# Prefix sums from a softplus split in two fp32r parts, with reordered loads, tokens and conversions, in a gated attention and MLP kernel

## The chip, the cores and the metric

The kernel runs on one core of one Trainium2 chip. The metric is the time of one execution on the device in microseconds; the median over three runs counts.

## What is computed

Per head, a gated linear attention with a state of 48 x 48: `state = f[t] * state + k[t] v[t]^T`, `y[t] = q[t] state`, with `f = 1 / (1 + exp(-f_logit))`; 4 batches, 8 heads, 768 tokens. The heads are joined to 384 channels. Then follows a token mix and a first MLP:

```
xt = x.transpose(0, 2, 1)
h = xt @ U @ V
u = x + h.transpose(0, 2, 1)
x = u + np.maximum(u @ w_ch1, 0.0) @ w_ch2
```

and a second MLP with a convolution of three taps over the tokens and a gate: `h = relu(x @ w_in)`, `out = (h * sigmoid(conv(h))) @ w_out`. The weights come in as 64-bit floats.

## The kernel before

**Chunks.** The attention runs over 24 chunks (6 per batch) of 128 tokens, in a loop over i. What is called chunk i below is iteration i. The logarithms of the gates are summed within a chunk by a matrix product with the triangle `tri`: `prefix(g)` multiplies `tri` by the softplus `sp` of chunk g into `n`, ScalarE makes `a = Exp(-n)` and `b = Exp(n)` of it, and `hats()` multiplies q by a and k by the clamped b (`qh`, `kh`), on VectorE for the first six chunks and on GpSimd from then on. `turn` transposes qh and kh on TensorE and ScalarE copies them out. `scores(i)` are eight products of keys and queries (`s`), `mask` multiplies them by the triangle on VectorE (`p`), and `out_chunk(i)` collects `y` in strips of 32 columns: first the queries with the state of the chunks before (`y<-qT,w`, not in the first chunk of a batch), then the masked scores with the values (`y<-p,v`), and last, unless the chunk is the last of its batch, the products `kv` that feed the next state. `state_end` adds kv to the state on VectorE (`wtmp`) and GpSimd scales it (`w`) by the prefix end of the chunk. That end is the last row of a; `ends` sends it to DRAM and `ends_back` fetches it over the partitions (`ga`).

**Tokens.** `tokens` transposes a finished chunk (`xt`, three transposes); ScalarE rounds it to fp32r (`xh`) and VectorE makes the rest (`xl`). `mix_in` multiplies both by U (`z`); when a batch is complete, `mix_z` prepares the sum and `mix_out` adds the product with V (`mix`), two products per chunk over three chunks.

**How values are split.** The large products run in fp32r, as three products of a high and a low part. `split` rounds on ScalarE (line 105) and subtracts on another engine (line 79). Products in plain fp32 are written as one `mm` call and appear in the trace as two matmuls.

**The order.** Every engine executes in program order, and the program is written out by hand, without a scheduler. In iteration i the loads of f for chunk i + 4, of k and q for i + 3 and of v for i + 2 are issued on SP first, then `ends_back`; `prefix(i + 2)` and `mix_next` follow, the scores, the hats, the masks, the token transposes, the transpose of the next queries, the gates (Exp and Ln of `f`, lines 547 and 548) of chunk i + 3, `ends(i + 2)`, `out_chunk`, and the transpose of the next keys between two mix products. `slot` deals out the steps that turn 64-bit weights into fp32r (VectorE, lines 128 to 138), some ahead of the masks and some behind the gates:

```
def slots(i):
    return (0, 6) if i == 1 else (0, 0) if i < 5 else (2, 2) if i < 8 else (1, 2)
```

**The seam.** In chunk 23 the first MLP's input is split; `up1` and `down1` follow, and `hooks` insert the last token mix between the products of the first `up1`. The two MLPs, some 504 us, run from fp32r parts throughout.

Of the kernel before, what the change touches and what calls it, by code (L numbers as in the profile page):

```python
# [35 lines left out]
def kernel(  # L36
# [168 lines left out]
    def mlps(ms, banks, pieces, late, checks, hooks):  # L205
# [226 lines left out]
        split1(0, 1, (nc.gpsimd, nc.vector))  # L432
        yield
# [60 lines left out]
    tri = gc.tile([128, 128], F32, name="tri")  # L494
    ga = gc.tile([128, NG, NP], F32, name="ga")
# [18 lines left out]
    sps = {}  # L514
# [34 lines left out]

    def prefix(g):  # L550
        n = bank(6, [128, DM], "n")
        mm(n, tri, sps.pop(g).rearrange("p h d -> p (h d)"), True, True)
# [108 lines left out]
    def out_chunk(g):  # L661
# [104 lines left out]
    with tc.manual_schedule():  # L766
# [7 lines left out]
        nc.vector.memset(ga, 1.0)  # L774
        for t, x in ((a_t[0], 1.0), (q_t[0], 0.0), (k_t[0], 0.0)):
# [58 lines left out]
        def slots(i):  # L834
            return (0, 6) if i == 1 else (0, 0) if i < 5 else (2, 2) if i < 8 else (1, 2)
# [31 lines left out]
        for i in range(1, NG):  # L867
            load_of(f"f{i + 4}")
            for x in "kq":
                load_of(f"{x}{i + 3}")  # L870
            load_of(f"v{i + 2}")
            if i < NG - 1:
# [3 lines left out]
            if EARLY_GATES <= i < NG - 3:  # L876
                gate_max(i + 3)
# [20 lines left out]
            if i < EARLY_GATES:  # L898
                gate_max(i + 3)
# [14 lines left out]
            if i < NG - 3:  # L914
                gates(i + 3)
# [233 lines left out]
```

## Time and profile before

| | |
|---|---|
| median of 3 runs | 654.48 us (653.5 to 655.22) |
| profiled execution, its own time | 654.5 us |
| its span | 652.8 us |
| TensorE busy | 641.3 us (98%) |
| VectorE / ScalarE / GpSimd busy | 424.9 / 275.2 / 145.6 us |
| granted TensorE clock | 0.998 of full speed |

The profile is one execution as the hardware recorded it. Busy time is the time in which an engine has at least one instruction under way; matrix products are pipelined, so a busy TensorE need not be one at its peak, and the distance between two like products tells more than their duration. PE is TensorE's product, PEld its weight load, DVE VectorE, ACT ScalarE, POOL GpSimd, SP the engine that issues the transfers. An idle time in square brackets stands before an instruction, with what ended it.

### The profile page before, as it was taken

How to read it: one execution, taken by the hardware profiler on the slowest of the kernel's cores; microseconds unless marked ns; L12 is line 12 of the kernel's file. 1: busy time of each engine (PE TensorE's matmuls, PEld its weight loads, DVE VectorE, ACT ScalarE, POOL GpSimd, SP SyncE). 2: the span in 40 equal slices, each digit the busy share in tenths (PEclk: the TensorE clock that was granted, in tenths of full speed). 3: DMA queues.
4: the chain of work that ended last, by engine and by line, in shares of the span. 5: the costliest groups of instructions: out<-in, count | busy, mean ns of one | idle time of the engine just before them, and what ended most of it. 6: DMA issues, size and time to landing. Idle time of an engine off the chain costs nothing.

```text
span 652.8 us, 12695 instructions
## 1 busy us (share of the span) xinstructions
PE 641.3 (98%) x5146; PEld 559.3 (86%) x5146; DVE 424.9 (65%) x663; ACT 275.2 (42%) x524; POOL 145.6 (22%) x181
## 2 busy tenths in 40 slices
PE   8999999999999999999999999999999999999995
PEld 6788778777888788888888888889999999999995
DVE  4868876566666665666665334226988777787762
ACT  5779677853223232222232111123544644634533
POOL 1176678441222222111112000001120110110000
PEclk9999999999999999999999999999999999999999
DMA  9988898810333330222220466100000200200202
GB/s 181 171 163 168 168 175 155 148 51 2 96 98 96 98 97 1 73 73 73 72 73 0 126 193 190 48 0 2 1 0 1 73 2 0 74 2 1 72 1 78
DMA packets 132661, 50.56 MB, mean 77 GB/s; under 512 B 112900, under 2 KB 128285, under 8 KB 132595
## 3 DMA queue, kind: packets, MB, share of 16 engines
q1 hardware_dynamic: 132594, 49.67, 31.2%
q8 instruction: 42, 0.69, 0.4%
q14 instruction: 25, 0.20, 0.1%
HBM read 44.89 MB, written 4.76 MB: 76 GB/s over the span
## 4 chain that ended last, share of the span: by engine, by line
PE 94%; DVE 2%; ACT 1%; issue 1%; DMA 0%; POOL 0%; POOLq 0%
PE a L76 38%; PE b L76 38%; PE y L76 5%; PE s L76 4%; PE n L76 2%; PE kTp L598 2%; PE xt L688 1%; PE qTp L598 1%; PE z L76 1%; PE mix L76 1%; PE kv L76 1%; DVE p L619 1%; DMA f<-in_f_logit_dram 0%; ACT sp L548 0%; PE row L76 0%
## 5 line engine op out<-in xcount | busy, mean ns | idle before, releaser
L262 ACT ACTIVATE rh<-a 128x512 fp32r<-128x512 f32 x72 | 43.1, 599 | 221.9 <-PE a L76 217.6
L263 DVE SCALAR_TENSOR_TENSOR rl<-a,rh 128x512 fp32r<-128x512 f32 x72 | 49.8, 692 | 109.1 <-ACT rh L262 109.0
L76 PE MATMUL a<-uh,w1l 128*128 128x512 f32 x216 | 84.4, 391 | 0.0
L76 PE MATMUL a<-uh,w1h 128*128 128x512 f32 x216 | 84.2, 390 | 0.0
L76 PE MATMUL a<-ul,w1h 128*128 128x512 f32 x216 | 84.1, 389 | 0.0
L76 PE MATMUL b<-rh,w2l 128*128 128x512 f32 x216 | 84.1, 389 | 0.0
L76 PE MATMUL b<-rh,w2h 128*128 128x512 f32 x216 | 84.0, 389 | 0.0
L76 PE MATMUL b<-rl,w2h 128*128 128x512 f32 x216 | 84.0, 389 | 0.0
L76 PE MATMUL b<-woh,w1h 128*128 128x384 f32 x264 | 70.4, 335 | 0.0
L318 ACT ACTIVATE c<-c 128x768 f32<-128x768 f32 x31 | 26.3, 847 | 62.4 <-DVE c L348 62.4
L76 PEld LDWEIGHTS a<-uh,w1l 128*128 128x128 f32 x216 | 40.5, 188 | 10.0 <-POOL w1l L79 1.8
L76 PE MATMUL a<-w2h,winh 128*128 128x384 f32 x192 | 49.0, 336 | 0.0
L76 PEld LDWEIGHTS b<-woh,w1h 128*128 128x128 f32 x264 | 48.0, 188 | 0.0
L76 PEld LDWEIGHTS b<-rh,w2h 128*128 128x128 f32 x216 | 40.6, 188 | 8.5
L76 PEld LDWEIGHTS b<-rh,w2l 128*128 128x128 f32 x216 | 40.5, 188 | 8.5
L76 PEld LDWEIGHTS b<-rl,w2h 128*128 128x128 f32 x216 | 40.5, 188 | 8.4
L76 PEld LDWEIGHTS a<-ul,w1h 128*128 128x128 f32 x216 | 40.6, 188 | 8.3
L76 PEld LDWEIGHTS a<-uh,w1h 128*128 128x128 f32 x216 | 40.6, 188 | 8.1
L79 POOL TENSOR_TENSOR ul<-u,uh 128x512 fp32r<-128x512 f32 (+1 forms) x15 | 19.1, 1295 | 127.0 <-ACT uh L105 127.0
L76 PE MATMUL b<-wol,w1h 128*128 128x384 f32 x132 | 44.3, 335 | 0.0
L304 ACT ACTIVATE h<-a 128x384 f32<-128x384 f32 x64 | 30.9, 496 | 29.3 <-PE a L76 26.0
L619 DVE TENSOR_TENSOR p<-s,tri 128x512 f32<-128x512 f32 x48 | 30.9, 686 | 17.9 <-PE s L76 17.6
(138 smaller groups left out, 1336.3 us busy)
## 6 DMA issues: line engine op xcount, KB each, us to landing
raw<-in_moe_w_ch_dram SPq DMA_DIRECT2D x48, 384.0 KB
f<-in_f_logit_dram SPq DMA_DIRECT2D x24, 192.0 KB
k<-in_k_dram SPq DMA_DIRECT2D x24, 192.0 KB
q<-in_q_dram SPq DMA_DIRECT2D x24, 192.0 KB
v<-in_v_dram SPq DMA_DIRECT2D x48, 96.0 KB
raw<-in_moe_w_in_dram SPq DMA_DIRECT2D x8, 384.0 KB
raw<-in_moe_w_out_dram SPq DMA_DIRECT2D x8, 384.0 KB
out_dram<-o SPq DMA_DIRECT2D x8, 192.0 KB
```

The source lines that it names most:

```text
L76: nc.tensor.matmul(out=out, lhsT=lhsT, rhs=rhs, start=start, stop=stop, skip_group_check=True)
L79: eng.tensor_tensor(out=out, in0=a, in1=b, op=ALU.subtract)
L262: nc.scalar.activation(out=rh, in_=ps, func=ACTF.Relu)
L263: nc.vector.scalar_tensor_tensor(out=rl, in0=ps, scalar=0.0, in1=rh.bitcast(F32), op0=ALU.max, op1=ALU.subtract)
L304: nc.scalar.activation(out=h[:, 1 + hf.start:1 + hf.stop], in_=ps, func=ACTF.Relu)
L318: nc.scalar.activation(out=c, in_=c, func=ACTF.Sigmoid)
L598: nc.tensor.transpose(out=ps[:, p, :], in_=src[:, p, 0:MP], identity=ident)
L619: nc.vector.tensor_tensor(out=t, in0=sc[g][j], in1=tri.unsqueeze(1).to_broadcast([128, NP, C]), op=ALU.mult)
L688: nc.tensor.transpose(out=ps[:, m * 128:(m + 1) * 128], in_=u32[:, m, g * C:(g + 1) * C], identity=ident)
```

## The change

- From chunk 13 on (`SPLIT_GATES`) the softplus is split on VectorE by `gate_split(i + 3)`, behind the masks and xl of chunk i: a cast into `sph` and a subtraction into `spl`. `prefix` multiplies both by `trir`, an fp32r copy of the triangle, in place of one fp32 product. Eleven chunks are treated so.
- From chunk 4 on, an iteration begins with `ends_back(i + 1)`, `prefix(i + 2)` and `ends(i + 2)`; the loads come behind. The loads of f run up to two chunks further ahead, those of k, q and v one, and so do the gates.
- The token transposes stand ahead of the scores instead of behind the masks.
- In the first chunk of a batch the products kv stand ahead of the strips.
- The conversion steps are dealt out by a table: 6 in chunk 1, 4 each in 5 to 7, 2 each in 8 to 10, 12 and 13, 1 each in 14 and 17 to 19, 4 each in 20 and 21.
- The last token transposes, the second half of the MLP's input split, and the reduction of the least gate move to other hooks at the seam.

```diff
+SPLIT_GATES = 13
+AHEAD = 4
...
+            def hook(kk):
+                hooks.pop((u, i, kk), int)()
+                if (u, i, kk) == (0, 0, 0):
+                    split1(0, 1, (nc.gpsimd, nc.vector))
...
+    def gate_split(g):
+        sp = sps.pop(g)
+        h_, l_ = [ga1.tile([128, DM], F32R, tag=t, name=t) for t in ("sph", "spl")]
+        src = sp.rearrange("p h d -> p (h d)")
+        nc.vector.tensor_copy(out=h_, in_=src)
+        sub(nc.vector, l_, src, h_.bitcast(F32))
+        sph[g] = h_, l_
...
-        mm(n, tri, sps.pop(g).rearrange("p h d -> p (h d)"), True, True)
+        if g in sph:
+            h_, l_ = sph.pop(g)
+            mm(n, trir, h_, True, False)
+            mm(n, trir, l_, False, True)
+        else:
+            mm(n, tri, sps.pop(g).rearrange("p h d -> p (h d)"), True, True)
...
+        if g % NCH == 0:
+            kv_of(g)
...
+        if g % NCH:
+            kv_of(g)
...
-            return (0, 6) if i == 1 else (0, 0) if i < 5 else (2, 2) if i < 8 else (1, 2)
+            return {1: (0, 6), 5: (2, 2), 6: (2, 2), 7: (2, 2), 8: (1, 1), 9: (1, 1), 10: (1, 1), 12: (1, 1), 13: (1, 1), 14: (0, 1), 17: (0, 1), 18: (0, 1), 19: (0, 1), 20: (2, 2), 21: (2, 2)}.get(i, (0, 0))
...
-            load_of(f"f{i + 4}")
-            for x in "kq":
-                load_of(f"{x}{i + 3}")
-            load_of(f"v{i + 2}")
-            if i < NG - 1:
+            if EARLY_GATES <= i < NG - 1:
+                ends_back(i + 1)
+            if EARLY_GATES <= i < NG - 2:
+                hats = prefix(i + 2)
+                ends(i + 2)
...
+            if i > 1 and not late_tokens:
+                lows.append(tokens(turned, 0 if i < NG - 2 else 6))
+                turned += 1
             scores(i)
...
-            lows = []
-            if i > 1:
-                lows.append(tokens(turned))
-                turned += 1
...
+            if SPLIT_GATES <= i + 3 < NG:
+                gate_split(i + 3)
...
-        tokens(NG - 1, 6)()
-        next(mlp)
...
         def last_casts():
+            last_ends()
             last["z"]()()
...
-        hooks.update({(0, 0, KD): last_z, (0, 1, 1): last_add, (0, 1, KD - 1): last_casts, (1, 0, 0): last_ends, (1, 0, 1): last_mix})
+        hooks.update({(0, 0, 0): lambda: tokens(NG - 1, 6)(), (0, 0, KD): last_z, (0, 1, 1): last_add, (0, 1, KD - 1): last_casts, (1, 0, 1): last_mix})
```

TensorE's order from the end of one chunk to the scores of the next, chunk 12 to 13, before the change:

```order
L76 MATMUL kv<-v_127,kh_124 32x48 x16
L598 MATMUL kTp<-ident,kh_125 112x128 [waits Activation_49,Pool_49]
L598 MATMUL kTp<-ident,kh_125 112x128 x3
L76 MATMUL n<-sp,tri 128x384 [waits Activation_49]
L76 MATMUL z<-xh,uhl 64x384
L76 MATMUL z<-xl,uhl 64x384 [waits DVE_49]
L76 MATMUL s_1835<-qT,kT 128x128 [waits Activation_49]
```

and with it:

```order
L78 MATMUL y<-p_1656,v_127 32x128 x7
L619 MATMUL kTp<-ident,kh_125 112x128 [waits Activation_49,Pool_49]
L619 MATMUL kTp<-ident,kh_125 112x128 x3
L78 MATMUL n<-sph,trir 128x384 [waits DVE_49]
L78 MATMUL n<-spl,trir 128x384 [waits DVE_49]
L78 MATMUL z<-xh,uhl 64x384
L78 MATMUL z<-xl,uhl 64x384
L715 MATMUL xt<-ident,u_76 128x128 x3
L78 MATMUL s_1744<-qT,kT 128x128 [waits Activation_49]
```

The product n waits for VectorE instead of ScalarE and is two products; the strips of p stand where kv stood; and xt has come in front of the scores.

VectorE's order in chunk 13, from the masks to the state's sum, before the change:

```order
L619 TENSOR_TENSOR p_1732<-s_1718,tri 128x512 [waits PE_49]
L619 TENSOR_TENSOR p_1734<-s_1719,tri 128x512 [waits PE_49]
L79 TENSOR_TENSOR xl<-xt,xh 128x384 [waits Activation_49]
L130 SCALAR_TENSOR_TENSOR cvt<-raw,cvt 128x384 [waits DVE_49]
L643 TENSOR_TENSOR wtmp<-kv,w_114 48x192 [waits PE_49]
```

and with it:

```order
L640 TENSOR_TENSOR p_1758<-s_1744,tri 128x512 [waits PE_49]
L640 TENSOR_TENSOR p_1760<-s_1745,tri 128x512 [waits PE_49]
L81 TENSOR_TENSOR xl<-xt,xh 128x384 [waits Activation_49]
L562 CAST sph<-sp 128x384
L81 TENSOR_TENSOR spl<-sp,sph 128x384 [waits DVE_49]
L664 TENSOR_TENSOR wtmp<-kv,w_115 48x192 [waits PE_49]
```

Between xl and the state's sum a conversion step has gone and the two instructions of the split have come.

SP's transfers of one chunk in the middle, before the change:

```order
L527 DMA f<-in_f_logit_dram 128x8x48 [waits Pool_49]
L527 DMA k<-in_k_dram 128x8x48 [waits DMAHW5_49,Pool_49]
L527 DMA q<-in_q_dram 128x8x48 [waits DMAHW6_49]
L523 DMA v_129<-in_v_dram 128x4x48 [waits DMAHW7_49,PE_49]
L523 DMA v_129<-in_v_dram 128x4x48 [waits DMAHW0_49,PE_49]
L584 DMA ga<-ends_d 112x4x1 [waits DMAHW3_49,DMAHW1_49]
L580 DMA ends_d<-a_118 1x512 [waits DMAHW2_49,Activation_49]
```

and with it:

```order
L605 DMA ga<-ends_d 112x4x1 [waits DMAHW4_49,DMAHW2_49]
L601 DMA ends_d<-a_120 1x512 [waits DMAHW3_49,Activation_49]
L533 DMA f<-in_f_logit_dram 128x8x48 [waits Pool_49]
L533 DMA k<-in_k_dram 128x8x48 [waits DMAHW5_49,Pool_49]
L533 DMA q<-in_q_dram 128x8x48 [waits DMAHW6_49]
L529 DMA v_128<-in_v_dram 128x4x48 [waits DMAHW7_49,PE_49]
L529 DMA v_128<-in_v_dram 128x4x48 [waits DMAHW0_49,PE_49]
```

The two transfers of the prefix ends, the second of which waits for ScalarE, now stand ahead of the loads.

## Rows read from the trace of the kernel before

**Rows 1.** The page: busy us (share of the span) x instructions.

```profile
PE 641.3 (98%) x5146; PEld 559.3 (86%) x5146; DVE 424.9 (65%) x663; ACT 275.2 (42%) x524; POOL 145.6 (22%) x181
```

**Rows 2.** The page: the chain that ended last, by engine.

```profile
PE 94%; DVE 2%; ACT 1%; issue 1%; DMA 0%; POOL 0%; POOLq 0%
```

**Rows 3.** Timeline of TensorE, scores only: start us, us, engine, operation.

```profile
84.99 1.16 PE L76 MATMUL s<-qT,kT 48*128 48x128 f32 x16
90.58 1.16 PE L76 MATMUL s<-qT,kT 48*128 48x128 f32 x16
...
103.42 1.16 PE L76 MATMUL s<-qT,kT 48*128 48x128 f32 x16
109.41 1.16 PE L76 MATMUL s<-qT,kT 48*128 48x128 f32 x16
...
138.81 1.16 PE L76 MATMUL s<-qT,kT 48*128 48x128 f32 x16
144.20 1.16 PE L76 MATMUL s<-qT,kT 48*128 48x128 f32 x16
```

**Rows 4.** Busy time by windows, second MLP: us, PE (x), PEld, DVE, ACT, POOL, clock, DMA, GB/s.

```profile
500.00:600.00 100.00, 100.00 (x578) 100.00 (x577) 77.84 (x91) 49.28 (x88) 10.26 (x6) 1.00 0.07 25
```

**Rows 5.** Timeline of TensorE's weight loads, those with idle before them.

```profile
60.26 0.30 PEld L76 LDWEIGHTS n<-sp,tri 128*128 128x128 f32 x2 [0.38 <-ACT sp L548]
...
81.96 0.38 PEld L76 LDWEIGHTS y<-p,v 128*32 128x32 f32 x16 [0.17 <-DVE p L619]
82.49 0.38 PEld L76 LDWEIGHTS y<-p,v 128*32 128x32 f32 x16 [0.16 <-DVE p L619]
...
86.99 0.59 PEld L76 LDWEIGHTS y<-qT,w 112*32 112x32 f32 x24 [0.17 <-DVE p L619]
...
92.70 0.14 PEld L76 LDWEIGHTS y<-qT,w 112*32 112x32 f32 x2 [0.30 <-POOL w L644]
93.28 0.48 PEld L76 LDWEIGHTS y<-qT,w 112*32 112x32 f32 x19 [0.44 <-POOL w L644]
...
148.56 0.31 PEld L688 LDWEIGHTS xt<-ident,u 128*128 128x128 f32 x3 [0.47 <-ACT u L683]
...
155.94 0.19 PEld L76 LDWEIGHTS mix<-vst,zst 96*128 96x128 f32 x1 [0.31 <-DVE g_least L973]
```

**Rows 6.** Timeline of chunk 13, from the end of its scores to the next n.

```profile
86.08 0.31 PEld L688 LDWEIGHTS xt<-ident,u 128*128 128x128 f32 x3
...
86.18 1.29 DVE L619 TENSOR_TENSOR p<-s,tri 128x512 f32<-128x512 f32 x2 [0.59 <-PE s L76]
86.35 0.46 PEld L598 LDWEIGHTS qTp<-ident,qh 128*112 128x112 f32 x4
...
87.39 0.55 DVE L79 TENSOR_TENSOR xl<-xt,xh 128x384 fp32r<-128x384 f32 x1
...
89.38 0.30 PEld L76 LDWEIGHTS n<-sp,tri 128*128 128x128 f32 x2
```

**Rows 7.** VectorE's groups by form, 10 to 150 us: count, busy us, mean ns, idle before.

```profile
L129 DVE SCALAR_TENSOR_TENSOR cvt<-raw,cvt 128x384 int32<-128x384 int32 x4 | 4.9, 1222 | 0.1
...
L565 DVE TENSOR_TENSOR kh<-k,b 128x384 f32<-128x384 f32 x5 | 2.8, 558 | 0.2
...
L128 DVE TENSOR_SCALAR cvt<-raw 128x384 int32<-128x384 int32 x4 | 2.4, 607 | 0.1
...
L563 DVE TENSOR_SCALAR b<-b 128x384 f32<-128x384 f32 x5 | 1.8, 353 | 0.0
```

**Rows 8.** GpSimd's groups by form, 10 to 150 us.

```profile
L565 POOL TENSOR_TENSOR kh<-k,b 128x384 f32<-128x384 f32 x18 | 18.8, 1043 | 1.5
```

**Rows 9.** SP's waits and timeline, and who waited for q (us, times, longest).

```profile
SPq L580 <- ACT a L556: 5.3, 2, 4.5
...
127.54 1.03 SPq L523 DMA_DIRECT2D v<-in_v_dram  x2
...
POOL qh L560 <- DMA q<-in_q_dram: 4.5, 5, 1.6
```

More of the change, by code (lines that the diff above doesn't have):

```diff
@@ L431, in mlps @@
         yield
-        split1(0, 1, (nc.gpsimd, nc.vector))
-        yield
         n1 = NT * J1
@@ L494 @@
     tri = gc.tile([128, 128], F32, name="tri")
+    trir = gc.tile([128, 128], F32R, name="trir")
     ga = gc.tile([128, NG, NP], F32, name="ga")
@@ L673, in out_chunk, with kv_of @@
                     for p in range(NP) for x in range(3)], started)
+        if g % NCH == 0:
+            kv_of(g)
         strips([part(3 * p + gr, vv[:, 128 * p + 32 * x:128 * p + 32 * (x + 1)], pp[j][:, p, :])
                 for x, gr, j in ((0, 0, 0), (1, 1, 0), (2, 1, 1), (3, 2, 1)) for p in range(NP)], started)
+        if g % NCH:
+            kv_of(g)
+        vt.pop(g)
+    def kv_of(g):
         if (g + 1) % NCH:
             strips(state(g), set())
-        vt.pop(g)
     yt = {}
@@ L774 @@
         nc.vector.memset(ga, 1.0)
+        nc.vector.tensor_copy(out=trir, in_=tri)
         for t, x in ((a_t[0], 1.0), (q_t[0], 0.0), (k_t[0], 0.0)):
@@ L867 @@
         for i in range(1, NG):
-            load_of(f"f{i + 4}")
-            for x in "kq":
-                load_of(f"{x}{i + 3}")
-            load_of(f"v{i + 2}")
-            if i < NG - 1:
+            hats = None
+            if EARLY_GATES <= i < NG - 1:
[3 more added lines that the diff above has]
+                ends(i + 2)
+            more = sum(i > x for x in (2, 4))
+            for g in sorted({i + 4 + sum(i > x + 1 for x in (2, 4)), i + 4 + more}):
+                load_of(f"f{g}")
+            for x in [f"k{i + 3}", f"q{i + 3}", f"v{i + 2}"] * (i <= AHEAD) + [f"k{i + 4}", f"q{i + 4}", f"v{i + 3}"] * (i >= AHEAD):
+                load_of(x)
+            if i < EARLY_GATES:
                 ends_back(i + 1)
@@ L875 @@
                 state_end(i - 1)
-            if EARLY_GATES <= i < NG - 3:
-                gate_max(i + 3)
+            ahead = [g for g, on in ((i + 3, i <= AHEAD), (i + 4, i >= AHEAD)) if on and g < NG]
+            if i >= EARLY_GATES:
+                for g in ahead:
+                    gate_max(g)
             follow = slot_end()
@@ L881 @@
                 next(mlp)
-            hats = prefix(i + 2) if 1 < i < NG - 2 else None
+            if 1 < i < EARLY_GATES:
+                hats = prefix(i + 2)
             if i != CATCH_UP + 1:
                 mix_next()
+            lows = []
+            late_tokens = i == CATCH_UP + 1
+            if i > 1 and not late_tokens:
+                lows.append(tokens(turned, 0 if i < NG - 2 else 6))
+                turned += 1
             scores(i)
-            if i == CATCH_UP + 1:
+            if late_tokens:
                 mix_next()
+                lows.append(tokens(turned))
+                turned += 1
             if hats and i >= EARLY_GATES:
@@ L898 @@
             if i < EARLY_GATES:
-                gate_max(i + 3)
+                for g in ahead:
+                    gate_max(g)
             if hats and i < EARLY_GATES:
                 hats()
-            lows = []
-            if i > 1:
-                lows.append(tokens(turned))
-                turned += 1
             if i + 1 < NG:
@@ L911 @@
                 step()
+            if SPLIT_GATES <= i + 3 < NG:
+                gate_split(i + 3)
             if zq:
                 zq[0] = zq[0]()
-            if i < NG - 3:
-                gates(i + 3)
+            for g in ahead:
+                gates(g)
             if i < FILL_FROM:
@@ L919 @@
                 prefix(3)()
-            if 1 <= i < NG - 2:
+            if 1 <= i < EARLY_GATES:
                 ends(i + 2)
```

3 lines of the change are left out of this document (2 added, 1 removed).

## The prediction

> **What bounds the kernel now.** I read the page's busy times first: TensorE is busy for 641.3 of 652.8 us, so an engine beside it matters only where TensorE waits for it [rows 1]. The chain of waits says the same: 94% of the chain that ended last is TensorE's own work [rows 2]. So time is won in two ways, by less work in TensorE's stream or by taking out one of its waits, and every wait that another engine gains counts only if TensorE stands at the end of it.
>
> The change lies in the attention stage, which ends with the token transposes at 148.56 [rows 5]; the two MLPs behind it keep their order. The yardstick there is the distance between the score products of neighbouring chunks in the timeline [rows 3]. A chunk with nothing special, 13, takes 90.58 - 84.99 = 5.59 us. Chunk 16, with two mix products more, takes 109.41 - 103.42 = 5.99. Chunk 22 has the two mix products and no prefix sum, and takes 144.20 - 138.81 = 5.39.
>
> The profiled execution took 654.5 us with a span of 652.8; the median of the runs is 654.48. The sum below is made against 654.5 and holds for the median as it stands. About 0.3%, 2.0 us, is what a measurement of this kernel can tell from no change.
>
> **The change part by part.**
>
> *The prefix sum in two parts.* Chunks 16 and 22 differ on TensorE by the product n alone, so n costs 5.99 - 5.39 = 0.60 us of the stream [rows 3]. In its place stand two fp32r products of the same 384 columns. The nearest row is the second MLP, where products of 384 columns, each with a 128x128 weight load, follow one another: 578 in 100 us, 0.173 us each [rows 4]. Two are 0.35, so a chunk wins 0.25, and 11 chunks (13 to 23) win 2.75. The other bound are the two mix products, 5.99 - 5.59 = 0.40 for a pair, which gives 0.20 a chunk or 2.2 in all. I take 0.173, since these two also stand back to back. The Trainium skill ("FP8 and Floating Point Precision", TensorE Precision Notes) says that true FP32 takes four passes through the array; two passes for four would leave half of 0.60, 0.30 a chunk, and 3.3 us in place of 2.75, so row and rule differ by the weight loads.
>
> *What VectorE pays for it.* Each of the 11 chunks adds a cast and a subtraction of 128x384, behind the masks and xl. The nearest rows are instructions of this size on VectorE in this stage: with one input 0.353 us, with two 0.558 [rows 7], together 0.91. The other bound are the weight conversions of the same stage, 0.607 and 1.222 [rows 7], together 1.83. In chunk 13 the scores start at 84.99, the masks at 86.18, and xl ends at 87.94 [rows 6]: the split can start 2.95 us behind the scores, and ends 3.86 to 4.78 behind them. The product n that now waits for it stood at 89.38, 4.39 behind. Moving the token transposes xt ahead of the scores takes 86.35 - 86.08 = 0.27 out of what stands between, so TensorE is ready for n at 4.12. An ordinary chunk (13, 14, 19) thus waits between nothing and 0.66; so do 11 and 17, which have two mix products but, as the last of their batches, no kv. I take 0.2, five times, 1.0. In the chunks that begin a batch (12 and 18) there is no product with the state, and TensorE is ready some 0.6 earlier, at about 3.5: the wait is 0.36 to 1.28, I take 0.5, twice, 1.0. In the other mixing chunks (10, 15, 16, 20) n comes 0.4 later, at 4.5: nothing to 0.28, I take nothing. Chunk 20 gets conversion steps on both sides of the masks besides: 0.607 + 1.222 + 0.558 = 2.4 us more for VectorE at the long durations, of which nothing or all may show; as it also carries the tokens of two chunks on TensorE, I take nothing. Together 2.0 us, with bounds of 0.7 and 9.4 (3.3 + 2.6 + 1.1 + 2.4). I stand nearer to the short durations, since GpSimd, whose instructions lengthen those of VectorE, will start its products earlier than before (its state product is behind fewer conversions) and be at the end of kh when the split starts.
>
> *The transposes xt ahead of the scores.* The same three transposes in another place: nothing by themselves. They fill the time in which kT is copied, and no longer stand between scores and masks; what covered the masks then is the transpose of q and the product with the state, which is enough, since the second mask ends 2.48 behind the scores [rows 6] and its strips come last.
>
> *kv ahead of the strips where a batch begins* (chunks 0, 6, 12, 18). In chunk 12 the strips wait 0.17 and 0.16 for the masks [rows 5], and kv follows. With kv in front both waits are covered: 0.33 a chunk, 1.3 for four. At 12 and 18 the split eats it again, as counted above.
>
> *Gates a chunk earlier, conversions dealt out anew, loads a chunk ahead.* Three waits should go: n in chunk 8 stood 0.38 for the logarithm, which now is made a chunk earlier; the product with the state in chunk 14 stood 0.30 and 0.44 for GpSimd, which makes that state and had been held by a late q. An idle of 0.17 before that product stands in other chunks too, as in 13, and stays, so I count 0.38 + 0.57 = 0.95 [rows 5]. The 40 conversion steps are the same in number. On SP each chunk has the same seven transfers; the two with the prefix ends now stand in front, and the loads behind them wait for the Exp of the same chunk. SP has waited for that Exp 5.3 us in all, 4.5 of it once at the end [rows 9], so little is queued there, and the loads have a chunk more of lead.
>
> *The seam to the MLP.* The last token transposes waited 0.47 for the copy of y and the last mix product 0.31 for a reduction [rows 5]; the one is moved behind the first three MLP products, the other a step forward. Both are covered then: 0.78.
>
> The sum: -2.75 - 1.3 - 0.95 - 0.78 = -5.8 us won, 2.0 given back, -3.8 us in all, and 654.5 - 3.8 = **650.7 us**.
>
> **The rivals.**
>
> *All of it is hidden.* The split always runs at 0.91 and n waits only at the beginning of a batch (0.36 twice). Then 5.8 - 0.7 = 5.1 us are won: 649.4, and with short waits gone that I did not count about 648. For it speaks that the chunks 11, 15 and 16 get no conversions at all; against it that GpSimd makes a kh of 1.04 us in every chunk [rows 8], about the time of the split.
>
> *The loads set the pace.* SP issues its loads one behind the other almost without a pause from the start to the last one at 127.54 [rows 9]. If the transfers, not TensorE, allow no more than this rate, a faster chunk only finds its q and k late: GpSimd already waited for q 4.5 us in five places [rows 9]. Then nothing is won before about 128 us, and what is left is the seam and one or two prefix sums, 0.78 + 0.5, less a wait of 0.2 or so in each of the last two: 653.6. Against it: with one chunk more of lead, a load that lands when it did before still lands in time.
>
> *Slower: VectorE and GpSimd hold each other up.* The split stands just where GpSimd makes kh. A conversion with two inputs took 1.222 us in this stage where 0.558 is the time of one alone [rows 7], so a split instruction can be held for most of a kh. If every split is held for one whole kh, it takes 0.91 + 1.04 = 1.95 and ends 4.90 behind the scores: waits of 0.78 five times, 1.4 twice and 0.4 four times are 8.3 us, against 5.8 won: 657.0. The point from which it is slower by over 0.3% is a split of 1.9. Held at both instructions, 3.0 us, it costs another 1.04 in 11 chunks: 668. I put this rival at 660. Against it: of the conversions of one input the mean is 0.607 [rows 7], so far from all are held, and where VectorE gets late, GpSimd's next products start later too, and the two move apart. The Trainium skill has this as a rule: "SBUF — State Buffer", Who interferes with whom, says that a cast, or an instruction with two SBUF inputs, and a GpSimd instruction that reads SBUF exclude each other for the whole instruction. By that rule the trace agrees where 1.222 stands beside 0.558.
>
> **How the numbers follow.** The forecast, the product's gain less moderate waits of VectorE (649.5 to 652.5), has 0.48. All hidden (below 649.5) has 0.18. The loads, or waits that eat the gain (652.5 to 656.5), have 0.22. Slower by the mutual holding has 0.12. The first two are faster by over 0.3%: 0.66; the third is the same: 0.22; the last slower: 0.12. The range reaches from 647.3, all hidden and more waits gone, to 655.5, where waits of 6.8 us eat the whole gain; the rest of their bound of 9.4 us lies in the tenth that is left out above, as is a tenth below.
>
> **What would show it.** The profile of the changed kernel should have 22 fp32r products n; mixing chunks such as 16 at 5.7 to 5.8 us and ordinary ones such as 13 at 5.3 to 5.6; weight loads of n that wait for spl, some tenths behind ordinary chunks and most behind 12 and 18; the waits of 0.38, 0.44, 0.47 and 0.31 gone; the seam some 3 us earlier. It is wrong if spl takes near 1.2 us on average, if n waits over half a us in mixing chunks, or if GpSimd waits for q more than the 4.5 us of before.

## The result, and the profile after

The changed kernel took **659.29 us** (median of 6 runs, 658.33 to 662.28), the kernel before 654.72 on the same chip (6 runs, 653.3 to 655.69). The ratio, which goes by all runs and not by the two medians alone, is 1.0080, with a 95% interval of 1.0055 to 1.0104. By the medians the change is slower by 4.6 us, at 659.3 where 650.7 was forecast. The profiled execution is the longest of the six: 662.28 us, with a span of 660.6. Its losses therefore add up to 7.8 us and not to 4.6.

The page of the changed kernel: span, busy times, the granted clock in 40 slices, and the chain that ended last, which answer to [rows 1, 2].

```profile
span 660.6 us, 12710 instructions
PE 642.1 (97%) x5146; PEld 561.7 (85%) x5146; DVE 434.4 (66%) x686; ACT 273.6 (41%) x524; POOL 144.8 (22%) x181
PEclk9997999999999999999999999999999999999998
...
PE 91%; DVE 4%; ACT 1%; issue 1%; DMA 1%; SPq 0%; POOL 0%; POOLq 0%; DVEq 0%
```

TensorE's share of the chain fell from 94 to 91%, VectorE's rose from 2 to 4%, a DMA appears, and slice four has a clock of 0.7. Where the time went is read from the score products, as in [rows 3]. The timeline of TensorE in the changed kernel, scores of chunks 6, 7, 8, then 13, 14, 16, 17, 20 and 21:

```profile
45.02 1.16 PE L78 MATMUL s<-qT,kT 48*128 48x128 f32 x16
53.24 2.08 PE L78 MATMUL s<-qT,kT 48*128 48x128 f32 x16 [3.14 <-ACT kT L621]
61.86 1.16 PE L78 MATMUL s<-qT,kT 48*128 48x128 f32 x16
...
91.61 1.16 PE L78 MATMUL s<-qT,kT 48*128 48x128 f32 x16
96.91 1.16 PE L78 MATMUL s<-qT,kT 48*128 48x128 f32 x16
...
109.23 1.16 PE L78 MATMUL s<-qT,kT 48*128 48x128 f32 x16
114.92 1.16 PE L78 MATMUL s<-qT,kT 48*128 48x128 f32 x16
...
131.32 1.16 PE L78 MATMUL s<-qT,kT 48*128 48x128 f32 x16
140.72 1.16 PE L78 MATMUL s<-qT,kT 48*128 48x128 f32 x16
```

And in the kernel before, scores of chunks 6, 7 and 8:

```profile
44.85 1.16 PE L76 MATMUL s<-qT,kT 48*128 48x128 f32 x16
49.88 1.16 PE L76 MATMUL s<-qT,kT 48*128 48x128 f32 x16
55.47 1.16 PE L76 MATMUL s<-qT,kT 48*128 48x128 f32 x16
```

Chunk 13 takes 5.30 us and chunk 16 5.69, as forecast (5.3 to 5.6, 5.7 to 5.8). But chunk 6 takes 8.22 (5.03 before), chunk 7 8.62 (5.59 before) and chunk 20 9.40 (7.34 before). Chunks 6 and 7 alone lose 6.2 us of the 7.8 by which the profiled span grew.

**The stall at chunks 6 and 7.** Timelines of SP, GpSimd (POOL), ScalarE and TensorE there:

```profile
44.44 1.42 SPq L120 DMA_DIRECT2D raw<-in_moe_V_dram  x3
46.82 2.07 SPq L533 DMA_DIRECT2D f<-in_f_logit_dram  x2
50.62 0.51 POOL L548 TENSOR_SCALAR sp<-f 128x384 f32<-128x384 f32 x1 [5.19 <-DMA f<-in_f_logit_dram]
51.16 0.52 ACT L553 ACTIVATE sp<-sp 128x384 f32<-128x384 f32 x1 [3.79 <-POOL sp L548]
52.60 0.59 ACT L621 COPY kT<-kTp 112x512 f32<-112x512 f32 x1
53.24 1.79 PEld L78 LDWEIGHTS s<-qT,kT 48*128 48x128 f32 x16 [3.37 <-ACT kT L621]
```

It is read from bottom to top. TensorE waits 3.37 us for ScalarE's copy of kT. ScalarE stands in its order behind the gates of chunk 10, which wait for GpSimd's maximum, which waits 5.19 for f of chunk 10. That f was issued at 46.82, behind the two sets of k, q and v that iteration 4 issues and behind V's raw words. Not all of the delay in that queue is bytes: between 36 and 47 us SP also waited 2.4 us for TensorE to give back buffers of v, 0.7 in the kernel before. The windows show what comes on top (columns as in [rows 4]):

```profile
50.00:55.00 5.00, 1.86 (x17) 1.76 (x16) 2.98 (x6) 3.39 (x8) 4.21 (x6) 0.79 0.82 152
55.00:60.00 5.00, 5.00 (x97) 4.13 (x95) 2.85 (x5) 3.03 (x6) 1.89 (x3) 0.52 1.04 218
```

The first of these windows in the kernel before:

```profile
50.00:55.00 5.00, 5.00 (x118) 4.35 (x118) 4.74 (x9) 4.35 (x9) 2.76 (x4) 1.00 0.98 202
```

Behind the idle time the granted clock falls to 0.52 on average, close to TensorE's lower level (1.2 of 2.4 GHz). The scores of chunk 7 take 2.08 us in place of 1.16, and the chunk 3.0 us more.

**The split beside GpSimd.** VectorE's subtraction in iterations 11 and 12, with GpSimd's product of k:

```profile
83.36 1.00 POOL L586 TENSOR_TENSOR kh<-k,b 128x384 f32<-128x384 f32 x1
83.52 1.25 DVE L81 TENSOR_TENSOR spl<-sp,sph 128x384 fp32r<-128x384 f32 x1
...
88.36 1.02 POOL L586 TENSOR_TENSOR kh<-k,b 128x384 f32<-128x384 f32 x1
89.94 0.56 DVE L81 TENSOR_TENSOR spl<-sp,sph 128x384 fp32r<-128x384 f32 x1
```

The same subtraction takes 1.25 us where it starts inside GpSimd's product, and 0.56 where that product is over. The groups of the three operations, each from the answer on its line or tile (count, ns least/median/most, first and last start, form):

```profile
L562 DVE CAST sph<-sp x11: 348/350/1182, 77.1 to 137.5; 128x384 fp32r<-128x384 f32 x11
...
L81 DVE TENSOR_TENSOR spl<-sp,sph x11: 557/559/1252, 77.5 to 138.7; 128x384 fp32r<-128x384 f32 x11
...
L81 DVE TENSOR_TENSOR xl<-xt,xh x14: 546/547/558, 76.7 to 148.8; 128x384 fp32r<-128x384 f32 x14
```

And the first two by form, 10 to 150 us, as in [rows 7] (busy us, mean ns, idle before):

```profile
L81 DVE TENSOR_TENSOR spl<-sp,sph 128x384 fp32r<-128x384 f32 x11 | 8.6, 779 | 0.4
L562 DVE CAST sph<-sp 128x384 fp32r<-128x384 f32 x11 | 6.0, 547 | 0.0
```

xl, a subtraction of the same size with one input in PSUM, never takes over 0.558. Chunk 20 has the split, four conversion steps and the mixing, and TensorE waits there again and again for a late VectorE, and once for ScalarE's copy (some of its weight loads with idle before them):

```profile
132.96 0.13 PEld L78 LDWEIGHTS z<-xl,uhl 128*64 128x64 f32 x1 [0.42 <-DVE xl L81]
...
135.52 0.38 PEld L78 LDWEIGHTS y<-p,v 128*32 128x32 f32 x16 [0.55 <-DVE p L640]
...
137.69 0.19 PEld L78 LDWEIGHTS mix<-vst,zst 96*128 96x128 f32 x1 [0.72 <-ACT u L710]
138.71 0.19 PEld L78 LDWEIGHTS n<-sph,trir 128*128 128x128 f32 x1 [0.21 <-DVE sph L562]
139.30 0.19 PEld L78 LDWEIGHTS n<-spl,trir 128*128 128x128 f32 x1 [0.41 <-DVE spl L81]
140.24 0.31 PEld L715 LDWEIGHTS xt<-ident,u 128*128 128x128 f32 x3 [0.52 <-DVE u L758]
```

### The profile page after: what moved, and what is told of

It reads as the page before. It is cut to its first block, busy times and chain, and to the rows that moved or that the text cites. A ratio compares the mean times of both kernels' runs of the same rounds, so it can differ in the third digit from the quotient of the medians.

```text
span 660.6 us, 12710 instructions
## 1 busy us (share of the span) xinstructions
PE 642.1 (97%) x5146; PEld 561.7 (85%) x5146; DVE 434.4 (66%) x686; ACT 273.6 (41%) x524; POOL 144.8 (22%) x181
## 4 chain that ended last, share of the span: by engine, by line
PE 91%; DVE 4%; ACT 1%; issue 1%; DMA 1%; SPq 0%; POOL 0%; POOLq 0%; DVEq 0%
PE a L78 38%; PE b L78 37%; PE y L78 4%; PE s L78 4%; PE n L78 2%; PE kTp L619 2%; PE qTp L619 1%; DVE p L640 1%; PE xt L715 1%; PE z L78 1%; PE kv L78 1%; PE mix L78 1%; DMA f<-in_f_logit_dram 1%; PE warm L78 1%; DVE zst L81 0%
```

## The experiments

Each kernel is measured against the kernel before on the same chip, whose median there lies between 656.02 and 656.53 us, so kernels are compared by their ratios; e8, a single execution, has none. The table has the length of each chunk in us, from one score product to the next in the timelines of the profiled executions (e1 to e13 are the runs told of below). Chunk j holds the split of the gates of chunk j+3 and their prefix product.

```
chunk before  after     e1     e2     e3     e4     e5     e6     e7     e8     e9    e10    e11    e12    e13
    6   5.03   8.22   5.02   5.60   9.04   7.89   6.29   5.02   5.01   9.01   5.10   5.02   5.01   5.02   9.42
    7   5.59   8.62   5.58   5.95   8.49   7.14   7.46   5.58   7.77   8.10   8.92   5.66   5.77   5.76   6.45
    8   5.98   5.59   5.97   5.58   5.58   5.58   5.58   6.38   5.98   5.58   6.34   6.24   6.03   6.18   5.98
    9   6.09   6.81   6.46   6.07   6.81   6.81   6.30   6.62   6.08   6.81   6.61   6.70   6.92   6.78   6.39
   10   6.70   5.70   6.15   5.70   5.70   6.00   5.70   5.70   6.47   5.70   5.69   5.69   6.00   5.70   6.91
   11   5.71   6.73   7.03   6.42   7.02   6.13   6.13   9.83   5.70   6.04   6.12   6.44   6.12   6.13   5.70
   12   5.04   4.92   5.55   5.54   4.91   5.01   5.83   4.93   5.02   4.91   4.91   5.67   5.02   5.23   5.02
   13   5.59   5.30   5.53   5.97   5.30   5.59   5.32   5.32   5.58   5.31   5.30   5.28   5.58   5.85   5.58
   14   6.28   5.33   6.62   5.33   5.32   5.59   5.32   5.33   5.86   5.33   5.32   5.32   5.59   5.59   5.85
   15   6.56   6.99   5.93   6.98   7.55   6.27   6.83   6.82   6.53   6.32   6.82   7.21   6.06   6.43   6.47
   16   5.99   5.69   6.21   5.70   5.70   6.00   5.75   5.74   6.00   5.92   5.75   5.69   6.00   5.73   6.00
   17   5.71   6.19   6.88   6.19   6.89   5.71   5.70   5.70   5.70   5.46   5.70   6.67   5.70   5.70   5.71
   18   5.03   4.91   5.53   4.91   4.91   5.01   5.13   5.11   5.02   4.91   5.30   4.91   5.02   5.02   5.02
   19   5.92   5.30   5.30   5.29   5.30   5.59   5.30   5.30   5.59   5.30   5.30   5.31   5.59   5.58   5.59
   20   7.34   9.40   9.88   9.40   8.24   8.41   7.52   7.52   7.72   8.57   7.51   7.48   7.23   7.24   7.72
   21   5.40   5.67   5.67   5.66   5.29   5.50   5.29   5.28   5.28   5.74   5.29   5.77   5.30   5.29   5.29
   22   5.39   5.37   5.36   5.36   5.38   5.38   5.37   5.38   5.38   5.36   5.37   5.37   5.36   5.36   5.36
 6-22  99.35 106.74 104.67 101.65 107.43 103.61 100.82 101.56 100.69 104.37 101.35 100.43  98.30  98.59 104.46
  6,7  10.62  16.84  10.60  11.55  17.53  15.03  13.75  10.60  12.78  17.11  14.02  10.68  10.78  10.78  15.87
 8-22  88.73  89.90  94.07  90.10  89.90  88.58  87.07  90.96  87.91  87.26  87.33  89.75  87.52  87.81  88.59
```

Chunks 6 and 7 must be read with care. e9 to e12 run the same instructions up to chunk 9, yet chunk 7 took 8.92 in e9 and 5.66 to 5.77 in the others; e2 and e5, alike up to there as well, differ by 2.2 us in the two. Even e7, whose loads stand at the old distances, has 7.77 in chunk 7: GpSimd waited 3.02 us for q there. The loads' arrival differs from execution to execution, so chunks 6 and 7 are judged by groups of kernels and by medians, the rest by the line 8-22.

**e1, distances as before.** The split goes behind the gates of its iteration.

```
-AHEAD = 4
+AHEAD = 99
...
-            for g in sorted({i + 4 + sum(i > x + 1 for x in (2, 4)), i + 4 + more}):
-                load_of(f"f{g}")
+            load_of(f"f{i + 4}")
...
-            if SPLIT_GATES <= i + 3 < NG:
-                gate_split(i + 3)
...
             for g in ahead:
                 gates(g)
+            if SPLIT_GATES <= i + 3 < NG:
+                gate_split(i + 3)
```

> The change with its loads and gates at the distances of the kernel before (f four chunks ahead, k and q three, v two, gates three), the split put behind the gates of its iteration. Theory A (the loss is the late f of chunk 10, because iterations 3 to 5 load an extra chunk while the transfers are full, and the gate's maximum on GpSimd, the gates on ScalarE and the kT copy behind them wait for it): chunks 6 and 7, which took 8.22 and 8.62 us in the changed kernel's trace, are back at 5.0 to 5.6 us, and the time falls by 4 to 6 us against 659.3, to 653 to 656 us. Rival B (the split's VectorE work and VectorE and GpSimd holding each other cost the time, from chunk 10 on): chunks 6 and 7 may shorten, but chunks 11 to 20 grow further since the split is now later against its use, and the time stays at 658 us or above.

Measured: 661.4 us, ratio 1.0089 (1.0069 to 1.0108). Theory A was right about chunks 6 and 7, which are back at 5.02 and 5.58, so they do hang on what runs ahead; it was wrong about the time. Rival B's forecast came in full: chunks 8 to 22 take 94.07 us in place of 89.90. Without gates that run ahead, VectorE waits for the logarithm before it can split (4.4 us in nine places), and n waits for the parts. The split needs the gates ahead, and the gates ahead need f.

**e2, one load moved.**

```
-                load_of(f"f{g}")
+                if g != 10:
+                    load_of(f"f{g}")
...
                 for g in ahead:
                     gate_max(g)
+            if i == 4:
+                load_of("f10")
```

> The change with one load moved: f of chunk 10 is issued in iteration 4 behind the two gate maxima, ahead of V's raw words, instead of in iteration 5. All other loads and gates still run ahead. Theory A (late f): the 5.19 us wait of GpSimd for f falls below 1 us, chunks 6 and 7 take under 6 us each, and the time falls by 3 to 5 us to 654 to 656.5 us. If the transfers as a whole are what is late (rival C: whatever is moved to the front, another load is late in its place), k, q or raw V words wait instead, chunks 6 to 8 keep 2 us or more of the loss, and the time is 657 us or above. Rival B (split and VectorE): no change of more than 1 us, 658 to 660 us.

Measured: 658.0 us, ratio 1.0035 (1.0014 to 1.0056), against 1.0080 for the change. More than half of the loss hung on the place of one load, by two ratios whose intervals just touch. Chunks 6 and 7 stay under 6 us, as theory A has it, but GpSimd still waits 3.17 us for f where A had under 1, and the median misses A's interval (654 to 656.5). e5, with the same loads, shows rival C: there V's raw words came late (VectorE waited 2.47 us for them), and chunk 7 took 7.46.

**e3, conversions spread.** The table of `slots`, from chunk 11 on:

```
-... 12: (1, 1), 13: (1, 1), 14: (0, 1), 17: (0, 1), 18: (0, 1), 19: (0, 1), 20: (2, 2), 21: (2, 2)}
+... 11: (0, 1), 12: (1, 1), 13: (1, 1), 14: (0, 1), 15: (0, 1), 16: (0, 1), 17: (1, 1), 18: (1, 1), 19: (1, 1), 20: (0, 1), 21: (0, 1)}
```

> The change with the conversion steps of chunks 20 and 21 (four each) dealt out to chunks 11, 15 to 19, one each, and one each left in 20 and 21. Theory A: chunk 20, 9.40 us in the changed kernel's trace against 7.34 before, falls by 1 to 1.5 us, chunks 15 to 19 pay back up to 0.5; time 658 to 659 us, since chunks 6 and 7 are untouched. Rival B (every VectorE operation beside the split costs its length): the steps cost as much where they go, time within 0.5 us of 659.3.

Measured: 662.05 us, ratio 1.0082 (1.0062 to 1.0103), as the change. Chunk 20 wins 1.16 and 21 0.38, but 11, 15 and 17 lose 0.29, 0.56 and 0.70; in 16, 18 and 19 a step costs nothing. In the sum rival B is right, as chunks 8 to 22 take 89.90 in both kernels. What it did not have is that the price of a step depends on the chunk.

**e4, no split.**

```
-SPLIT_GATES = 13
+SPLIT_GATES = 24
```

> The change with no chunk split: all prefix sums stay a product of float32, and VectorE has neither the cast nor the subtraction; all that runs ahead stays. Theory A (the split by itself gains 0.25 us in 11 chunks, of which about 2 us of waits for its parts are given back): time within 1 us of 659.3, chunks 6 and 7 as long as in the changed kernel. Rival B (the split's work on VectorE is the loss): the time falls by 2 us or more, to 657 us or below, the gain in chunks 10 to 20.

Measured: 661.02 us, ratio 1.0073 (1.0054 to 1.0092). The ratio says theory A, the table says why: the split wins 0.3 in chunks 10, 13, 14, 16 and 19, 0.1 in 12 and 18, and loses 0.60, 0.72, 0.48, 0.99 and 0.17 in 11, 15, 17, 20 and 21.

**e8, GpSimd's product left out in four chunks.**

```
-            eng.tensor_tensor(out=heads(k_t[g % 3]), in0=kt.pop(g), in1=b_, op=ALU.mult)
+            kt_g = kt.pop(g)
+            if g not in (13, 17, 19, 22):
+                eng.tensor_tensor(out=heads(k_t[g % 3]), in0=kt_g, in1=b_, op=ALU.mult)
```

> The change without GpSimd's product of k and its factor for chunks 13, 17, 19 and 22, which it does in iterations 11, 15, 17 and 20 while VectorE splits; the keys of these chunks are left out of the computation. Theory A2 (VectorE is held by that product): the cast takes 0.35 us and the subtraction 0.56 in these iterations instead of 0.57 to 1.18 and up to 1.25, the waits of the prefix product for its parts in them go, and the four chunks fall by 0.3 to 0.7 us each. Rival (VectorE is late there by the length of its queue, masks, subtractions and mixing): the operations stay as long and the chunks fall by under 0.2 us.

One execution: 658.83 us. Chunks 11, 15, 17 and 20 fall by 0.69, 0.67, 0.73 and 0.83 against the change, and chunks 8 to 22 by 2.6 in all. GpSimd and VectorE in iteration 11, and VectorE in iteration 15, in e8:

```profile
83.22 0.51 POOL L584 TENSOR_SCALAR b<-b 128x384 f32<-128x384 f32 x1
83.28 0.66 DVE L562 CAST sph<-sp 128x384 fp32r<-128x384 f32 x1
83.97 0.56 DVE L81 TENSOR_TENSOR spl<-sp,sph 128x384 fp32r<-128x384 f32 x1
...
106.11 0.35 DVE L562 CAST sph<-sp 128x384 fp32r<-128x384 f32 x1
```

The subtraction of iteration 11 took 1.25 in the change, the cast of iteration 15 1.18 (at 106.35 there). So VectorE is held, and its queue alone does not explain these chunks. What is left of GpSimd holds it still: the cast at 83.28 starts inside the limiting of b and ends 0.21 us behind it.

**e7, the order alone.** e1, with these edits besides:

```
-SPLIT_GATES = 13
+SPLIT_GATES = 24
...
-            return {1: (0, 6), 5: (2, 2), ...
+            return (0, 6) if i == 1 else (0, 0) if i < 5 else (2, 2) if i < 8 else (1, 2)
```

> The kernel before with the order of the change alone: the prefix product and its ends at an iteration's start, the token transposes ahead of the scores, the state's products ahead of the strips at batch starts, the seam's order; no split, loads, gates and conversions as before. The prediction had 1.3 us for the state's products and 0.78 for the seam, some 2 us in all: ratio 0.997. Theory D (the token transposes lay in the time that the masks need, and the state's products take their place there, so that the sum is nil): chunks 12 and 18 stay at 5.0 us and ordinary chunks at 5.6; ratio 0.999 to 1.001.

Measured: 656.65 us, ratio 1.0006 (0.9993 to 1.0019). Theory D holds. TensorE's timeline of chunk 12 in the kernel before and in e7:

```profile
79.95 1.16 PE L76 MATMUL s<-qT,kT 48*128 48x128 f32 x16
...
83.41 0.65 PE L598 MATMUL kTp<-ident,kh 128*112 128x128 f32 x4
```

```profile
82.20 1.16 PE L78 MATMUL s<-qT,kT 48*128 48x128 f32 x16
...
83.87 0.55 PE L78 MATMUL kv<-v,kh 128*32 128x48 f32 x32
...
85.31 0.65 PE L619 MATMUL kTp<-ident,kh 128*112 128x128 f32 x4
...
86.80 0.49 PE L715 MATMUL xt<-ident,u 128*128 128x128 f32 x3
```

kv starts in the time in which the masks are made, and the keys' transpose kTp, which comes behind kv and y, starts 85.31 - 82.20 = 3.11 us behind the scores in place of 83.41 - 79.95 = 3.46. But xt stood in that time before, and now takes 87.22 - 86.80 = 0.42 of its own, ahead of the next scores, which start at 87.22. Chunk 12 takes 5.02 us, 5.04 before.

**e13, k, q and v ahead alone.** In e7:

```
+LOADS = 4
...
-            for x in [...] * (i <= AHEAD) + [f"k{i + 4}", f"q{i + 4}", f"v{i + 3}"] * (i >= AHEAD):
+            for x in [...] * (i <= LOADS) + [f"k{i + 4}", f"q{i + 4}", f"v{i + 3}"] * (i >= LOADS):
```

> As e7 (the order of the change alone), with one edit: the loads of k, q and v run a chunk ahead from iteration 4 on, as in the change; f, gates and conversions stay as in the kernel before, and nothing is split. Theory C (the extra chunk of loads, 576 KB here, is paid once because the transfers are full): chunks 6 to 8 take 2 to 4 us more than in e7's trace would be without its own wait (16.6 us for chunks 6 to 8 in the kernel before, so 18.6 to 20.6 us), and the median lies 2 to 3.5 us over e7's: ratio 1.003 to 1.006. Rival A (loads that run ahead cost nothing by themselves, it is the gates a chunk earlier that stop ScalarE): within 0.8 us of e7, ratio 0.999 to 1.002.

Measured: 659.47 us, ratio 1.0044 (1.0027 to 1.0060). By the median and the ratio this is theory C: 2.8 us over e7 by the medians, 2.5 by the ratios, with nothing else changed. Chunks 6 to 8 of the profile take 21.85, over C's 18.6 to 20.6. Timelines of GpSimd and TensorE in e13:

```profile
50.63 0.60 POOL L549 TENSOR_SCALAR sp<-f 128x384 f32<-128x384 f32 x1 [4.87 <-DMA f<-in_f_logit_dram]
...
52.49 0.30 PEld L79 LDWEIGHTS n<-sp,tri 128*128 128x128 f32 x2 [3.67 <-ACT sp L555]
...
54.73 2.02 PE L79 MATMUL s<-qT,kT 48*128 48x128 f32 x16
```

The same stall and the same slower scores of chunk 7, though no gate runs ahead here: this time it is f of chunk 9. What makes f late are the loads in front of it. This is the window from 25 to 130 us of the kernel before:

```profile
25.00:130.00 105.00, 104.35 (x2038) 83.91 (x2034) 76.68 (x141) 81.37 (x169) 67.76 (x94) 1.00 0.86 165
```

The transfers are 0.86 busy and move 165 GB/s. The 576 KB of one more k, q and v take some 3.6 us at that rate (an estimate from this row), and the change brings forward two f of 192 KB besides, 960 KB in all or 6.0 us. That the profile of the change lost 6.2 us at chunks 6 and 7 is no proof of this sum: only 3.2 of it is the stall, and the six kernels with the same 960 KB ahead from iteration 4 on (the change, e2, e3, e4, e5, e8) lost between 0.9 and 6.9 us there in their profiles. How much of a late f is bytes and how much is SP's wait for v's buffers no run separates. Between 36 and 47 us that wait is 1.0 to 2.9 us in the kernels with this lead and 0.7 to 1.9 in those without, and the transfers moved as much there in the change as before it (161 and 163 GB/s), so the bytes are the likelier part.

**e5 and e6, two ways to fix the change.** Both keep the split for the prefix sums of 13, 15, 16, 17, 19, 21 and 22 only, and take the conversions out of chunk 20. e5 has the load order of e2 besides; e6 has in its place `AHEAD = 9` and `(7, 9)` for `(2, 4)` in the loads of f.

```
-            if SPLIT_GATES <= i + 3 < NG:
+            if i + 3 in SPLIT_GATES:
...
-... 14: (0, 1), 17: (0, 1), 18: (0, 1), 19: (0, 1), 20: (2, 2), 21: (2, 2)}
+... 14: (1, 1), 16: (1, 1), 17: (0, 1), 18: (1, 1), 19: (1, 1), 21: (2, 1)}
```

> Three edits on the change: f of chunk 10 first (as in the second run), the split kept only for the prefix sums of chunks 13, 15, 16, 17, 19, 21 and 22 and left out for 14, 18, 20 and 23, and the conversion steps taken out of chunk 20 and put into 14, 16, 18, 19 and 21. Theory A2 (the split gains 0.3 us where GpSimd is idle behind the masks, and costs 0.5 to 1.0 us in chunks 11, 15, 17 and 20, where its two VectorE operations run while GpSimd does a product of k, and VectorE is held): from the span of the second run, 655.8 us, minus 0.3, 0.7, 0.5 and 1.0 us in chunks 11, 15, 17 and 20, and minus 1 us in chunk 20 for the conversions: a span near 652.4, 2 us under the kernel before of the same chip (ratio 0.995 to 0.998). Rival B2 (the chunks' lengths follow from the state of all queues, and what leaves one chunk comes back in the next): ratio 1.000 or above.

> As e5, but instead of moving one load, the loads and gates run a chunk ahead from iteration 9 on instead of from 4 (f doubled in iterations 8 and 10). Theory A: the extra chunk of loads is then paid after V's raw words are in; chunks 6 and 7 take 5.0 and 5.6 us as in the kernel before, a gain of 0.9 us over e5, and no wait of GpSimd for f over 2 us appears at chunks 10 to 12; ratio 0.994 to 0.997. Rival C (the transfers are full in every chunk, so the stall comes wherever the extra loads are put): chunks 9 to 12 lengthen by 2 us or more in place of 6 and 7, ratio 1.000 or above.

Measured: e5 657.01 us, ratio 1.0009 (0.9991 to 1.0027); e6 658.22 us, ratio 1.0025 (1.0007 to 1.0042). Both ratios lie over the intervals of A2 and A. In the sum the edits on VectorE's side did nearly what A2 says: chunks 8 to 22 take 87.07 in e5, 3.0 us under e2, where A2 had 3.5, though chunk 15 fell by 0.15 and not by 0.7. The loads ate it again, by 3.1 us at chunks 6 and 7 in the profile of e5. In e6 chunks 6 and 7 are clean, and chunk 11 takes 9.83, by rival C. GpSimd and TensorE there in e6:

```profile
79.16 0.51 POOL L548 TENSOR_SCALAR sp<-f 128x384 f32<-128x384 f32 x1 [2.86 <-DMA f<-in_f_logit_dram]
81.28 0.19 PEld L78 LDWEIGHTS mix<-vst,zst 96*128 96x128 f32 x1 [2.31 <-ACT u L710]
```

**e9, e10, e11, only f and the gates ahead.** As e6, but k, q and v keep the distances of before. The split is for seven chunks in e9, for all eleven in e10 (`SPLIT_GATES = 13`), for none in e11 (`24`).

```
-            more = sum(i > x for x in (7, 9))
-            for g in sorted({i + 4 + sum(i > x + 1 for x in (7, 9)), i + 4 + more}):
+            for g in [i + 4] * (i < AHEAD) + [i + 5] * (i >= AHEAD - 1):
                 load_of(f"f{g}")
-            for x in [...] * (i <= AHEAD) + [f"k{i + 4}", f"q{i + 4}", f"v{i + 3}"] * (i >= AHEAD):
+            for x in (f"k{i + 3}", f"q{i + 3}", f"v{i + 2}"):
                 load_of(x)
```

> As e6 (split for seven chunks, conversions out of chunk 20), but only f and the gates run a chunk ahead, from iteration 8 and 9 on; k, q and v keep the distances of the kernel before. That loads 192 KB ahead of time in all, against 960 KB in the change (one chunk of k, q, v and two of f). Theory C, as it now stands (the transfers are 0.8 to 0.9 busy up to chunk 20, so what is loaded ahead is paid once, wherever it is put: 3.1 us at chunks 6 and 7 in e5, 3.7 us at chunk 11 in e6): with a fifth of the bytes no chunk from 6 to 12 takes 1.5 us more than in the kernel before, chunk 11 falls from 9.83 to 6.5 us or less, and the span is 651.5 to 653; ratio 0.994 to 0.998. Rival (gates that run ahead stop ScalarE at a late f in any case): a wait of GpSimd for f over 2.5 us remains at chunks 9 to 12, and the ratio is above 1.000.

> As e9, with the split for all of the chunks 13 to 23. Theory A2 (VectorE is held by GpSimd's product of k in chunks 11, 15, 17, 20): slower than e9 by 1.5 to 3 us, in these chunks. Rival: within 0.7 us of e9.

> As e9, with no split at all. Theory A2 (0.28 us gained in each of the chunks 10, 13, 14, 16 and 19 and 0.1 in 12 and 18): slower than e9 by 1 to 2 us, each of these five chunks at 5.6 us (10 and 16 at 6.0) in place of 5.3 (5.7). Rival (the split gains nothing in the sum): within 0.5 us of e9.

Measured: e9 655.41 us, ratio 0.9994 (0.9980 to 1.0008); e10 656.99 us, 1.0018 (1.0004 to 1.0032); e11 654.33 us, **0.9973 (0.9962 to 0.9984)**. With a fifth of the bytes chunk 11 is back at 6.12 (theory C), though e9's ratio lies over C's interval and chunk 7, at 8.92, breaks its bound; GpSimd waited 2.46 us for q there. No wait of GpSimd for f over 2.5 us is left at chunks 9 to 12, so the rival does not hold either. The full split costs 1.6 us against the seven chunks (e10 and e9, within A2's 1.5 to 3) and 2.7 against none, by the medians. But A2 has e11 slower than e9 by 1 to 2 us, and it is not: on chunks 8 to 22, where no chance stall is in it, e9 takes 87.33 and e11 87.52. Seven chunks won 0.2 us together.

**e12, the split of four chunks.** In e9:

```
-SPLIT_GATES = (13, 15, 16, 17, 19, 21, 22)
+SPLIT_GATES = (13, 15, 16, 19)
```

> As e11 (f and the gates alone run ahead, conversions out of chunk 20, no split), with the split for the prefix sums of chunks 13, 15, 16 and 19 alone: those whose two VectorE operations and whose neighbours in e9 met no product of GpSimd (chunks 10, 12, 13 and 16 took 5.69, 4.91, 5.30 and 5.75 us there, against 6.00, 5.02, 5.58 and 6.00 in e11). Theory A2: 0.9 us under e11, a ratio of 0.994 to 0.997 and chunk 15 at 6.1 us. Rival (what the split gains comes back in the next chunk): ratio 0.997 to 0.999.

Measured: 655.6 us, ratio 0.9981 (0.9966 to 0.9995), within the rival's interval; chunk 15 takes 6.43, not 6.1. Chunks 10 and 16 win 0.3 each, but 12 and 13, which were free in e9, lose 0.2 and 0.3. The trace shows this in iteration 12 of e12:

```profile
83.51 1.02 POOL L581 TENSOR_TENSOR qh<-q,a 128x384 f32<-128x384 f32 x1 [2.10 <-DMA q<-in_q_dram]
84.78 0.75 DVE L81 TENSOR_TENSOR spl<-sp,sph 128x384 fp32r<-128x384 f32 x1
85.21 1.20 POOL L586 TENSOR_TENSOR kh<-k,b 128x384 f32<-128x384 f32 x1
85.45 1.36 DVE L131 SCALAR_TENSOR_TENSOR cvt<-raw,cvt 128x384 int32<-128x384 int32 x1
```

GpSimd got its q late, so its product of k fell on VectorE's operations: the subtraction took 0.75 and the conversion step behind it 1.36. Where VectorE is free of GpSimd is not a property of the chunk, it follows from when loads land. e11 is the best version found: the change's order, f and gates a chunk ahead, its conversions out of chunk 20, and no split.

## Why the prediction was wrong

- **The product n, 2.75 us won.** The mechanism and its size were right, 0.28 to 0.30 us in each chunk where nothing waits (13: 5.58 against 5.30 in e11 and e9), where 0.25 was taken. The Trainium skill ("FP8 and Floating Point Precision", TensorE Precision Notes) states four passes for true FP32, from which the prediction estimated 0.30; the trace agrees with that better than with the row of the second MLP. But the gain shows in full in five chunks and by a third in two, 1.7 us in all, and not in eleven.
- **"The loads have a chunk more of lead", costed at nothing: this is the step that failed.** I looked for waits on SP's queue and did not look at the transfers themselves, 0.86 busy. More lead had to be paid first, 960 KB in a stage that moves 165 GB/s, and the bill fell on the first instruction with a short lead, f of chunk 10. In the profile it was 6.2 us, 3.2 of it the stall of chunk 6 and 3.0, nearly all, the slower clock behind it. In the medians e7 to e13 show 2.8 for k, q and v alone, and e9 to e6, which differ in the loads alone, 2.8 as well (2.5 and 2.0 by the ratios). The rival on the loads named the resource and still gave the lead away for nothing, so its worst was "nothing is won". SP's wait for the Exp, put at little, came to 15.7 us in ten places, but only 0.3 of it lies between 25 and 50 us, so it is not what made this stall.
- **What VectorE pays, 2.0 us: too little, and in the wrong places.** The split of all chunks costs 1.3 us in the sum (e4 against the change), which is 1.7 won and 3.0 given back, where the prediction had 0.75 won. With 0.29 gained by n in each of eleven chunks, 3.2 in all, VectorE took back 4.5. Ordinary chunks (13, 14, 19), put at 0.2 each, paid nothing. The mixing chunks 15 and 20, put at nothing, and 11 and 17, put at 0.2, lost 0.5 to 1.0 beyond their gain. I stood near the short durations, 0.91 together; they took 0.547 + 0.779 = 1.33 on average, the least being 0.348 and 0.557. "The two move apart" did not happen in chunks 11, 15, 17 and 20.
- **The rival "slower", 660 us.** Its total came close to 659.3, mostly by another cause. Its mechanism is real: e8 takes it away in four chunks and wins 0.7 to 0.8 us in each. The Trainium skill ("SBUF — State Buffer", Who interferes with whom) says that a VectorE instruction with at most one SBUF input, outside the two-port modes, does not contend with GpSimd. The trace agrees: xl, with one input in PSUM, took 0.546 to 0.558 fourteen times, also at 82.36, where GpSimd's product of q ran from 81.66 to 82.68, while spl took up to 1.252.
- **kv ahead of the strips, 1.3 us: nil** (e7: chunks 12 and 18 at 5.02). I counted xt's new place at nothing because its old place had been in the shade of the masks too; taking xt out of that shade and putting kv in it exchanges one for the other, 0.35 for 0.42. In chunks 17 and 20 of the change xt then waited 0.52 for the mix product's addition.
- **Waits of 0.38 and 0.57 gone: right.** Chunk 8 took 5.59 in place of 5.98, and chunk 14 5.59 without the split (6.28 before). With the order alone (e7) chunk 8 stays at 5.98 and chunk 14 comes to 5.86, so part of the second gain is not the earlier gates'.
- **The seam, 0.78: nil.** From the last scores to the first product b of the MLP the changed kernel has 164.13 - 151.76 = 12.37 us, the kernel before 156.92 - 144.20 = 12.72 [rows 3]. But one set of the transposes xt, 0.4, now stands ahead of these scores. The two waits left their places, and new ones of 0.27, 0.28 and 0.41 came.
- **Conversions in chunk 20, "nothing or all may show".** About 1 us showed: chunk 20 takes 8.41 in e4, without the split, and 7.23 in e11, where the steps are out of it too.
- **The signs.** Two of the three signs of being wrong stayed away: spl took 0.78 on average, and GpSimd no longer waits for q at all. The third came: n waited 0.64 and 0.62 us for its parts in the mixing chunks 15 and 20. No sign looked at f, for which GpSimd waited 6.8 us in two places between 10 and 150 us, and 4.0 before the change.

Taken together, the forecast missed the median by 8.6 us. About 5 of it are the split (2.1), kv (1.3), the seam (0.8) and the conversions (1.0), by the profiles. By this rough subtraction some 3.5 are left for the loads, the largest single term. The pairs of kernels above, 2.0 to 2.8, come near that size; the 6.2 of the one profile, the longest execution, is more than the median lost.

## What to carry to other kernels

Before a load is moved earlier, read the transfers' own busy share over the stage. Here it was 0.86, and a longer lead was not free: it came due at the first transfer that had no lead to spare, and engines that work in program order handed that wait on to TensorE. The bytes divided by the rate of the stage, 6.0 us, gave the order of the cost and not its size, which was 0.9 to 6.9 us in the profiles. And an operation that gains on the busiest engine by work on VectorE has to be costed per chunk against what GpSimd does at that moment, at the held duration as well as the short one.

## What was not expected of the hardware

A wait of TensorE of 3.4 us cost nearly twice its length: the granted clock was 0.79 in the window of the wait and 0.52 in the one behind it, with every product at about half speed (scores 2.08 us, 1.16 otherwise). And how late a load lands differs from one execution to the next: with identical instructions up to there, chunk 7 took 8.92 us in e9 and 5.66 in e10. Whether that comes from the memory or from the order in which the sixteen engines take up transfers was not tried.
